# Moving 47 of 76 groups of transposes of a fused attention and token-mixing kernel from TensorE to the DMA crossbar, with a new order of the program

## The chip, the cores and the metric

One core of one Trainium2 chip. The metric is the device time of one execution in microseconds (us). Lower is better. The profile of one execution goes with each kernel; its span is 1 to 2 us shorter than the measured time.

## The reference

```python
# q, k, v: (8, 12, 448, 64) fp32;  moe_w_q, moe_w_k: (768, 64);  moe_w_out: (768, 768)
scores = q @ k.T / sqrt(64) - log(448)
x = sigmoid(scores) @ v                      # per batch and head, then heads side by side: (8, 448, 768)
wq, wk = x @ w_q, x @ w_k
W = wq @ wk.T / sqrt(64)                     # (8, 448, 448)
out = maximum(W @ x, 0) @ w_out
```

## The kernel before

Work goes by 24 "pairs": two batches by two heads. Each pair loads q, k and v (448 KB each, on SP's queue), casts them to bf16 on GpSimd (POOL), transposes q and k on TensorE (seven 128x128 blocks into PSUM, then a VectorE copy), and makes seven score blocks, each followed by one sigmoid over 128x896 on ScalarE. After six pairs the MLP of two batches follows, among the scores of the next pairs; it needs x transposed too. The order of everything is a string, one letter per step: S a score block with its sigmoid, P its product with v, q and k a transpose group, x a transpose of x, W N U M the MLP, O an output block.

```python
    def tr(n, nm, split=False):                       # q or k by TensorE
        fb, ps = bank([P, NI, 2, NP], BF16, "pt" + nm)
        t16 = ld.pop((nm + "16", n))
        for i in range(NI):
            nc.tensor.transpose(ps[:, i]..., t16[:, i]..., ident16)
        t = p_qk.tile([P, 2, NI, NP], BF16, tag=nm + "t", name=nm + "t")
        ...                                           # one VectorE copy PSUM -> t

    def pump_loads():                                 # loads: three buffers each for q, k, v
        while len(loaded) < len(ORDER):
            nm, n = ORDER[len(loaded)]
            ...
                if n >= 3 and (nm, n - 3) not in cast:
                    break
                load1(n, nm, nc.sync)
            loaded.add((nm, n))

    def pump():                                       # casts, and behind each cast the next load
        while len(cast) < len(ORDER) + 2:
            nm, n = ORDER[len(cast) - 2]
            ...
                cast1(n, nm, nc.gpsimd)
            cast.add((nm, n))
            pump_loads()
    # (cuts are marked by ...)
```

Of the kernel before, what the change touches and what calls it, by code (L numbers as in the profile page):

```python
# [9 lines left out]
F32 = mybir.dt.float32  # L10
BF16 = mybir.dt.bfloat16
# [5 lines left out]
def kernel(  # L17
# [41 lines left out]
    p_c16 = pool("c16", 2)  # L59
    p_v16 = pool("v16", 3)  # L60
    p_qk = pool("qk", 8)
# [23 lines left out]
    wqk32 = singles.tile([P, H, P], F32, name="wqk32")  # L85
# [41 lines left out]
    def tr(n, nm, split=False):  # L127
        fb, ps = bank([P, NI, 2, NP], BF16, "pt" + nm)
        t16 = ld.pop((nm + "16", n))
        for i in range(NI):  # L130
            nc.tensor.transpose(  # L131
                ps[:, i].rearrange("p h n -> p (h n)"),
                t16[:, i].rearrange("p b d -> p (b d)"), ident16,
            )
        t = p_qk.tile([P, 2, NI, NP], BF16, tag=nm + "t", name=nm + "t")

        def evac(hs):
            nc.vector.tensor_copy(  # L138
                out=t[:, hs], in_=ps[:, :, hs, :].rearrange("p i h n -> p h i n")
            )  # L140
        qk[nm, n] = t
        free1.append(fb)
        if split:
            return evac
        evac(slice(0, 2))
# [4 lines left out]
    def scores(n, i):  # L150
        fb, sc = bank2("sc")
        for b2 in range(2):
            for h in range(2):
                nc.tensor.matmul(  # L154
                    sc[HALF[h], b2, 0:S], qk["k", n][HALF[b2], h, i, :],
                    qk["q", n][HALF[b2], h].rearrange("p i n -> p (i n)"), start=True, stop=True,
                )
        at = p_at.tile([P, 2, S], BF16, tag="at", name="at")
        nc.scalar.activation(at, sc[:, :, 0:S], ACTF.Sigmoid, bias=bias_t, scale=attn_scale)  # L159
        free2.append(fb)  # L160
        ats[n, i] = at
# [21 lines left out]

    def tr_x(n):
        u, j = pairs[n]
        if j == 0:
            xns[u] = p_x.tile([P, 4, 2, D], BF16, tag="xn", name="xn")
        fb, ps = bank([P, 4, 2, 2, HD], BF16, "px")
        for h in range(2):
            for m in range(4):  # L190
                nc.tensor.transpose(  # L191
                    ps[:, m, h].rearrange("p b d -> p (b d)"), xts[j][:, h, m * P : (m + 1) * P],
                    ident16,
                )
        for b2 in range(2):
            nc.vector.tensor_copy(  # L196
                out=xns[u][:, :, b2, 2 * HD * j : 2 * HD * (j + 1)].rearrange(
                    "p m (h d) -> p m h d", h=2
                ),
                in_=ps[:, :, :, b2, :],  # L200
            )
        free1.append(fb)

# [4 lines left out]
    def mlp_wqk(u, h):  # L208

        if h == 0:  # L210
            pw[u] = bank2("pw")
        fb, ps = pw[u]
        for b2 in range(2):
            for x in range(2):
                nc.tensor.matmul(  # L215
                    ps[HALF[x], b2, 0:S], wqk16[HALF[b2], h, 64 * x : 64 * x + 64],
                    xts[h // 2][HALF[b2], h % 2, 0:S], start=(h == 0), stop=(h == H - 1),
                )
        if h == H - 1:
            nc.vector.tensor_copy(out=wqk[:, :, 0:S], in_=ps[:, :, 0:S])  # L220
            free2.append(fb)

    def mlp_wkn(u):
        fb, ps = bank([P, 4, 2, P], BF16, "pk")
        for b2 in range(2):
            for m in range(4):
                nc.tensor.transpose(ps[:, m, b2, :], wqk[:, b2, m * P : (m + 1) * P], ident16)  # L227
        wkn[u] = p_one.tile([P, 4, P], BF16, tag="wkn", name="wkn")
        nc.vector.tensor_copy(
            out=wkn[u], in_=ps.rearrange("p m b x -> p m (b x)")[:, :, 64:192]  # L230
        )
        free1.append(fb)

    def mlp_tmp(u, nb, act):
        if nb == 0:
            tmps[u] = p_one.tile([P, D], BF16, tag="tmp", name="tmp")
        fb, ps = bank([P, NB], F32, "pt")
        for m in range(4):
            for b2 in range(2):
                nc.tensor.matmul(  # L240
                    ps[HALF[b2]], wkn[u][:, m, 64 * b2 : 64 * b2 + 64],
                    xns[u][:, m, b2, nb * NB : (nb + 1) * NB],
                    start=(m == 0), stop=(m == 3),
                )
        dst = tmps[u][:, nb * NB : (nb + 1) * NB]
        if act:
            nc.scalar.copy(out=dst, in_=ps)
        else:
            nc.vector.tensor_copy(out=dst, in_=ps)
        free1.append(fb)  # L250
# [75 lines left out]
    def load_weights():  # L326
        for b2 in range(2):
            for x, w in enumerate((moe_w_q, moe_w_k)):
                o = 64 * (x ^ b2)
                nc.sync.dma_start(  # L330
                    out=wqk32[HALF[b2], :, o : o + 64], in_=w.rearrange("(h d) n -> d h n", d=HD)
                )
# [4 lines left out]


# [12 lines left out]
    nc.sync.dma_start(out=q0, in_=src["q"])  # L351
    nc.sync.dma_start(out=k0[:, :, cols(KA)], in_=src["k"][:, :, cols(KA)])
    nc.sync.dma_start(out=k0[:, :, cols(KB)], in_=src["k"][:, :, cols(KB)])
# [9 lines left out]
    fb, ps = bank2("pwarm")  # L363
    for _ in range(32):
        nc.tensor.matmul(ps[:, 0, 0:P], zeros, zeros, start=True, stop=True)
    free2.append(fb)
# [4 lines left out]
    ORDER = [("q", 1), ("k", 1), ("v", 0)]  # L371
    nq = 2
    for n in range(1, N):
        for _ in range(2 if n in (1, 2, 3, 4) else 1):
            if nq < N:
                ORDER += [("q", nq), ("k", nq)]
                nq += 1
        ORDER.append(("v", n))
    for n, at_ in ((0, 18), (1, 30), (2, 33), (3, 36), (4, 39), (5, 42), (6, 45)):
        ORDER.insert(at_, ("w", n))  # L380
# [15 lines left out]
    def pump():  # L396

        while len(cast) < len(ORDER) + 2:
            nm, n = ORDER[len(cast) - 2]
            if (nm, n) not in loaded:  # L400
                break
            if nm == "w":
                if n:
                    nc.gpsimd.tensor_copy(out=wout16[:, n - 1, :], in_=w32[n - 1])
                else:
                    nc.gpsimd.tensor_copy(out=wqk16, in_=wqk32)
            else:
                back = 3 if nm == "v" else 2
                if n >= back and (nm, n - back) not in used:
                    break  # L410
                cast1(n, nm, nc.gpsimd)
            cast.add((nm, n))
            pump_loads()
# [11 lines left out]
    for nm in "qk":  # L425
        qk[nm, 0] = p_qk.tile([P, 2, NI, NP], BF16, tag=nm + "t", name=nm + "t")

    def tr_part(nm, t16, r, e, b=None):
        shape = [P, r.stop - r.start, 2, NP]
        fb, ps = (None, ps_q.tile(shape, BF16, tag=b, name="pt" + nm)) if b else bank(shape, BF16, "pt" + nm)  # L430
        for i in range(r.start, r.stop):
            nc.tensor.transpose(
                ps[:, i - r.start].rearrange("p h n -> p (h n)"),
                t16[:, i].rearrange("p b d -> p (b d)"), ident16,
            )
        COPY[e](out=qk[nm, 0][:, :, r], in_=ps.rearrange("p i h n -> p h i n"))
# [4 lines left out]
    tr_part("q", q016, IB, "s")  # L441
    tr_part("k", k016, KA, "v", free2[-1])
    used |= {("q", 0), ("k", 0)}
    pump()





    PLAN = (  # L450
        "SSSKqSSSSkq",
        "SPPPPPSkSSPkSPqSS",
        "SxPqSPPPPSPPSqSPPSkPSPP",
        "SxPSSPkSSSkPPSkP",
        "SPPPPSqSqSSqxSxSk",
        "SSqkPPSPPPPSPqSkSSxPPPP",
        "SPPPSkqSWWWSWWWWSWWWWSWSx",
        "SNPSPPPPSPPSUSqSMUmSMq",
        "SkSMxSkSPPPSPPPPSqSk",
        "SMxmqSPPPPSPPPSOSSSOO",  # L460
        "SSkxSSOkSPPPSPPPPSO",
        "SSSqOkSPPPSPPPPSqxSPPPP",
        "SPPPSOSSSqOxSWWWWWSWW",
        "SWWWWWSOSSSNxPPPPPSPPSUU",
        "SMSxkSPPPPSPPPSOSMSkO",
        "SMmOkSMSOqSMSqOSPPPPSPPP",
        "SOSSSkOxSPPPSPPPPSxO",
        "SSSOOSSxOSPPSPPPPPPPPP",
        "SPPPSxqSWSWWWWWWSWWWSWWOS",
        "SSONSSOxSPPPPPPSPSUU",  # L470
        "SSMxOSSPPPPPPPSOSMSkx",
        "SPPPSPPPPmOSMmqOSMSOqSS",
        "SkOxSPPPPSPPPSOSSSOOx",
        "SPSPPPPPPSOSSSOOxS",
        "WPPPWPPPPWWWWWWWWWWOONxOUUMmmOOmMmOOOOOOOOOOOOOOOO",
    )
    done = dict.fromkeys("SPqkKxWNUMO", 0)
    done["q"] = done["k"] = 1

    for t in "".join(PLAN).replace(" ", ""):  # L480
        kind = "M" if t == "m" else t
# [5 lines left out]
        elif t == "P":  # L487
            n, i = divmod(c, NI)
            values(n, i)
            if i == NI - 1:  # L490
                used.add(("v", n))
                pump()
        elif t in "qk":
            tr(c, t)
            used.add((t, c))
            pump()
        elif t == "K":
            tr_part("k", k016, KB, "v")
        elif t == "x":
            tr_x(c)  # L500
        elif t == "W":
            mlp_wqk(*divmod(c, H))
        elif t == "N":
            mlp_wkn(c)
# [38 lines left out]
```

## Time and profile before

| | before |
|---|---|
| time | 210.34 us median of 2 runs (210.27 to 210.42) |
| span, granted clock of the profiled run | 209.4 us, 0.984 |
| first sigmoid starts, last one ends | 6.5 us, 177.7 us |
| ScalarE waits between them | 14.7 us, for scores (the stretch less its work; the page's own count of the waits before sigmoids, used for the other kernels below, is 12.6 us) |
| tail after the last sigmoid | 31.7 us |

The chain that ended last, by engine:

```profile
PE 75%; DMA 16%; POOL 2%; SPq 1%; ACT 1%; issue 1%; DVE 1%; DVEq 0%; ACTq 0%; POOLq 0%
```

### The profile page before, as it was taken

How to read it: one execution, taken by the hardware profiler on the slowest of the kernel's cores; microseconds unless marked ns; L12 is line 12 of the kernel's file. 1: busy time of each engine (PE TensorE's matmuls, PEld its weight loads, DVE VectorE, ACT ScalarE, POOL GpSimd, SP SyncE). 2: the span in 40 equal slices, each digit the busy share in tenths (PEclk: the TensorE clock that was granted, in tenths of full speed). 3: DMA queues.
4: the chain of work that ended last, by engine and by line, in shares of the span. 5: the costliest groups of instructions: out<-in, count | busy, mean ns of one | idle time of the engine just before them, and what ended most of it. 6: DMA issues, size and time to landing. Idle time of an engine off the chain costs nothing.

```text
span 209.4 us, 6320 instructions
## 1 busy us (share of the span) xinstructions
PE 197.0 (94%) x2630; PEld 117.5 (56%) x2630; DVE 121.9 (58%) x208; ACT 170.8 (82%) x193; POOL 72.6 (35%) x85
## 2 busy tenths in 40 slices
PE   8498988889999999999999999999999999999991
PEld 7254544556546656656656565655565555655561
DVE  2135555755598746664889675645788654554321
ACT  3689999979999999999998989889898998055220
POOL 2477755577877842730022700251110000000000
PEclk9759999999999999999999999999999999999999
DMA  5999999999999999997065463355203252154785
GB/s 174 374 381 380 381 173 290 381 384 384 383 384 383 379 381 385 399 389 253 5 199 130 145 181 79 78 147 195 51 29 78 75 152 70 27 134 104 200 203 174
DMA packets 28684, 47.59 MB, mean 227 GB/s; under 512 B 5360, under 2 KB 24432, under 8 KB 28656
## 3 DMA queue, kind: packets, MB, share of 16 engines
q1 hardware_dynamic: 27616, 45.03, 67.1%
q10 hardware_dynamic: 1040, 2.16, 2.7%
q8 instruction: 20, 0.33, 0.7%
q14 instruction: 8, 0.07, 0.1%
HBM read 36.18 MB, written 11.01 MB: 225 GB/s over the span
## 4 chain that ended last, share of the span: by engine, by line
PE 75%; DMA 16%; POOL 2%; SPq 1%; ACT 1%; issue 1%; DVE 1%; DVEq 0%; ACTq 0%; POOLq 0%
PE po L283 27%; PE sc L154 15%; PE pv L173 13%; DMA v<-in_v_dram 9%; DMA k<-in_k_dram 8%; PE px L191 5%; PE pw L215 3%; PE ptq L131 3%; PE ptk L131 3%; PE pt L240 3%; PE pm L264 2%; ACT at L159 1%; POOL k L118 1%; POOL v L118 1%; SPq L107 1%; PE pk L227 1%
## 5 line engine op out<-in xcount | busy, mean ns | idle before, releaser
L159 ACT ACTIVATE at<-sc,bias_t 128x896 bf16<-128x896 f32 x168 | 155.4, 1020 | 12.6 <-PE sc L154 11.7
L283 PE MATMUL po<-wout,mx 128*128 128x384 bf16 (+1 forms) x342 | 60.6, 324 | 0.0
L154 PE MATMUL sc<-qt,kt 64*64 64x448 bf16 x672 | 57.7, 367 | 2.5 <-ACT at L159 1.8
L283 PEld LDWEIGHTS <-mx 128*128 128x128 bf16 x342 | 30.9, 98 | 24.3 <-issue 7.0
L173 PE MATMUL pv<-at,v 64*64 64x448 bf16 x672 | 41.8, 352 | 1.1 <-POOL v L118 1.1
L178 DVE CAST xt<-pv 128x896 bf16<-128x896 f32 x24 | 26.2, 1091 | 23.4 <-PE pv L173 23.4
L308 DVE COPY o<-po 128x384 f32<-128x384 f32 x45 | 25.1, 557 | 24.7 <-PE po L283 24.4
L154 PEld LDWEIGHTS <-kt 64*64 64x64 bf16 x672 | 21.9, 105 | 23.7 <-issue 12.6
L118 POOL CAST q<-q 128x896 bf16<-128x896 f32 x23 | 21.5, 933 | 33.3 <-issue 26.3
L118 POOL CAST v<-v 128x896 bf16<-128x896 f32 x24 | 22.3, 934 | 22.6 <-PE pv L173 18.0
L118 POOL CAST k<-k 128x896 bf16<-128x896 f32 x23 | 21.5, 933 | 19.4 <-PE ptk L131 15.7
L173 PEld LDWEIGHTS <-v 64*64 64x64 bf16 x672 | 20.5, 107 | 11.2 <-POOL v L118 1.4
L138 DVE COPY kt<-ptk 128x896 bf16<-128x896 bf16 x23 | 14.3, 620 | 10.3 <-PE ptk L131 10.2
L196 DVE COPY xn<-px 128x512 bf16<-128x512 bf16 x48 | 18.0, 417 | 2.9 <-PE px L191 2.9
L306 ACT COPY o<-po 128x384 f32<-128x384 f32 x10 | 4.8, 478 | 15.7 <-PE po L283 15.7
L256 DVE TENSOR_SCALAR mx<-pm 128x896 bf16<-128x896 f32 x15 | 16.3, 1088 | 1.8 <-PE pm L264 1.4
L138 DVE COPY qt<-ptq 128x896 bf16<-128x896 bf16 x23 | 14.1, 619 | 4.5 <-PE ptq L131 3.7
L131 PE MATMUL ptq<-ident,q 128*128 128x128 bf16 x161 | 13.7, 228 | 1.4 <-POOL q L118 1.4
L191 PE MATMUL px<-ident,xt 128*128 128x128 bf16 x192 | 14.7, 220 | 0.2 <-DVE o L308 0.2
L191 PEld LDWEIGHTS <-xt 128*128 128x128 bf16 x192 | 11.6, 98 | 4.6 <-issue 3.8
L131 PE MATMUL ptk<-ident,k 128*128 128x128 bf16 x161 | 13.3, 224 | 0.6 <-POOL k L118 0.6
L131 PEld LDWEIGHTS <-q 128*128 128x128 bf16 x161 | 9.9, 102 | 6.7 <-issue 3.7
(43 smaller groups left out, 93.8 us busy)
## 6 DMA issues: line engine op xcount, KB each, us to landing
q<-in_q_dram SPq DMA_DIRECT2D x24, 448.0 KB, 8.0
v<-in_v_dram SPq DMA_DIRECT2D x24, 448.0 KB, 7.5
k<-in_k_dram SPq DMA_DIRECT2D x23, 448.0 KB, 7.8
out_dram<-o SPq DMA_DIRECT2D x44, 192.0 KB, 3.0
w<-in_moe_w_out_dram SPq DMA_DIRECT2D x6, 384.0 KB, 5.8
out_dram<-o ACTq DMA_DIRECT2D x10, 192.0 KB, 3.2
wqk<-in_moe_w_q_dram SPq DMA_DIRECT2D x2, 192.0 KB, 9.4
wqk<-in_moe_w_k_dram SPq DMA_DIRECT2D x2, 192.0 KB, 8.5
```

The costliest lines, as they stand in the source:

```text
L118: eng.tensor_copy(out=t16.rearrange("p i b d -> p b i d"), in_=ld.pop((nm, n)).rearrange("p b (i d) -> p b i d", i=NI),)
L131: nc.tensor.transpose(ps[:, i].rearrange("p h n -> p (h n)"), t16[:, i].rearrange("p b d -> p (b d)"), ident16,)
L138: nc.vector.tensor_copy(out=t[:, hs], in_=ps[:, :, hs, :].rearrange("p i h n -> p h i n"))
L154: nc.tensor.matmul(sc[HALF[h], b2, 0:S], qk["k", n][HALF[b2], h, i, :], qk["q", n][HALF[b2], h].rearrange("p i n -> p (i n)"), start=True, ...
L159: nc.scalar.activation(at, sc[:, :, 0:S], ACTF.Sigmoid, bias=bias_t, scale=attn_scale)
L173: nc.tensor.matmul(ps[HALF[b2], h, 0:S], ld["v16", n][HALF[h], i, b2, :], ats[n, i][HALF[h], b2, :], start=(i == 0), stop=(i == NI - 1),)
L178: nc.vector.tensor_copy(out=xts[j][:, :, 0:S], in_=ps[:, :, 0:S])
L191: nc.tensor.transpose(ps[:, m, h].rearrange("p b d -> p (b d)"), xts[j][:, h, m * P : (m + 1) * P], ident16,)
L196: nc.vector.tensor_copy(out=xns[u][:, :, b2, 2 * HD * j : 2 * HD * (j + 1)].rearrange("p m (h d) -> p m h d", h=2), in_=ps[:, :, :, b2, :],)
L256: nc.vector.tensor_scalar(dst, ps, moe_scale, 0.0, ALU.mult, ALU.max)
L283: nc.tensor.matmul(ps, mxs[u][c].rearrange("p b s -> p (b s)")[:, m * P : (m + 1) * P], wout16[:, c, w0:w1], start=(c == 0), stop=(c == NC ...
L308: nc.vector.tensor_copy(out=o[:, nb * NB : (nb + 1) * NB], in_=ps)
```

## The change: intent and diff

TensorE was busy 94% of the span. The change takes from it the transposes of q and k of pairs 10 to 23 (28 groups), 18 of the 24 of x, and one of the MLP's, and lets the DMA crossbar do them from SBUF to SBUF, issued by SP right behind the cast. Less TensorE and VectorE work lets the program be replanned so that ScalarE never waits. The layouts of the transposed tiles change so that one DMA can write each; two more buffers for q and k, and one more for their casts; small changes of the start (first loads in halves on two queues, dummy matmuls); the MLP's two small weights are read once in place of twice.

```diff
-    p_c16 = pool("c16", 2)
+    p_c16 = pool("c16", 3)
-    p_qk = pool("qk", 8)
+    p_qk = pool("qk", 10)
...
+    def tr_dma(n, nm):
+        t16 = ld.pop((nm + "16", n))
+        t = p_qk.tile([P, NI, P], BF16, tag=nm + "t", name=nm + "t")
+        nc.sync.dma_start_transpose(out=t, in_=t16.rearrange("p i b d -> p (i b d)"))
+        qk[nm, n] = t
...
+    def tr_x_dma(n):
+        u, j = pairs[n]
+        nc.sync.dma_start_transpose(
+            out=xn_of(u, j).rearrange("p h m x -> p (h m) x"),
+            in_=xts[j].rearrange("p h s -> p (h s)"),
+        )
...
+    BY_DMA, AHEAD = 10, 3
+    PLAN = ( ... a new string; D = dummy matmuls, X = x by DMA, n = the MLP's by DMA ... )
...
+        elif t == "S" and seen[t] % NI == 0:          # loads of q and k: three pairs ahead of the scores
+            while seen["x"] < min(N, seen[t] // NI + AHEAD + 1):
+                ORDER += [("k", seen["x"]), ("q", seen["x"])]
+                seen["x"] += 1
...
                 cast1(n, nm, nc.gpsimd)
+                if by_dma:
+                    tr_dma(n, nm)
+                    used.add((nm, n))
             cast.add((nm, n))
             pump_loads()
```

## The prediction

> **What bounds the kernel now.** I read the page first for busy shares, then the timeline of ScalarE and of TensorE, then the waits of the DMA queue, and last the groups of the operations that the change touches. Busy shares and slices of the page:
>
> ```profile
> PE 197.0 (94%) x2630; PEld 117.5 (56%) x2630; DVE 121.9 (58%) x208; ACT 170.8 (82%) x193; POOL 72.6 (35%) x85
> ...
> PE   8498988889999999999999999999999999999991
> PEld 7254544556546656656656565655565555655561
> DVE  2135555755598746664889675645788654554321
> ACT  3689999979999999999998989889898998055220
> POOL 2477755577877842730022700251110000000000
> PEclk9759999999999999999999999999999999999999
> DMA  5999999999999999997065463355203252154785
> ```
>
> Two engines lead. TensorE is never idle after slice 10. ScalarE is full from slice 4 to about 20 (21 to 105 us), then drops a tenth here and there until slice 34, where the sigmoids are over and only TensorE works. DMA is full to slice 18 (95 us), then under half. So there are three stages: a start, a long stretch in which the 168 sigmoids run, and a tail of TensorE work that needs the last sigmoids.
>
> The first and the last sigmoids, from the ScalarE timeline (start, length, engine, line, count, idle before it):
>
> ```profile
> 6.47 2.80 ACT L159 ACTIVATE at<-sc,bias_t 128x896 bf16<-128x896 f32 x3 [0.76 <-PE sc L154]
> 11.04 3.70 ACT L159 ACTIVATE at<-sc,bias_t 128x896 bf16<-128x896 f32 x4 [1.77 <-PE sc L154]
> ...
> 16.16 26.25 ACT L159 ACTIVATE at<-sc,bias_t 128x896 bf16<-128x896 f32 x29 [0.25 <-PE sc L154]
> ...
> 170.39 2.80 ACT L159 ACTIVATE at<-sc,bias_t 128x896 bf16<-128x896 f32 x3 [0.39 <-PE sc L154]
> 173.49 2.80 ACT L159 ACTIVATE at<-sc,bias_t 128x896 bf16<-128x896 f32 x3 [0.30 <-PE sc L154]
> 176.69 1.01 ACT L159 ACTIVATE at<-sc,bias_t 128x896 bf16<-128x896 f32 x1 [0.39 <-PE sc L154]
> ```
>
> The reader sees the unhindered pace in the run of 29: 26.25 / 29 = 0.905 us each. 168 of them need 152 us. They took 177.7 - 6.5 = 171.2 us. Five ReLU activations of about 0.9 us stand among them (4.5 us); the other 14.7 us is ScalarE waiting, nearly always for TensorE's scores, from 0.2 to 1.8 us at a time. From there to the end of the span are 209.4 - 177.7 = 31.7 us. So TensorE sets the time from about 85 us on, with ScalarE close behind: relieving TensorE can win those 14.7 us, and no more than that in this stretch unless ReLUs also leave ScalarE.
>
> The groups that go:
>
> ```profile
> L196 DVE COPY xn<-px 128x512 bf16<-128x512 bf16 x48 | 18.0, 417 | 2.9 <-PE px L191 2.9
> L138 DVE COPY kt<-ptk 128x896 bf16<-128x896 bf16 x23 | 14.3, 620 | 10.3 <-PE ptk L131 10.2
> L131 PE MATMUL ptq<-ident,q 128*128 128x128 bf16 x161 | 13.7, 228 | 1.4 <-POOL q L118 1.4
> L191 PE MATMUL px<-ident,xt 128*128 128x128 bf16 x192 | 14.7, 220 | 0.2 <-DVE o L308 0.2
> ```
>
> Their durations overlap in TensorE's pipeline, so I don't multiply by 220 ns. I took instead, over TensorE's timeline, the time from a group's first start to the start of the next group, less idle time: 46 complete groups of 7 q or k transposes hold TensorE 0.44 to 0.47 us each over the run (0.40 to 0.45 after 30 us, at the full clock), and a group of 8 x transposes 0.52 us.
>
> **What the Trainium skill says.** "DMA: Bandwidth & Descriptors", section Latency and other measured facts, gives a DMA transpose 261 GB/s in one kernel and 350-400 when contiguous; its section Anatomy of one DMA gives every DMA about 2 us of fixed time. From these an estimate for one 224 KB q or k (0.9 us of data) is about 3 us to landing. "VectorE: DVE Perf Modes", section The three transpose paths, has 1309 ns for one 128x128 through the crossbar against 390 ns on TensorE: alone the DMA is slower, so the change pays only if it runs ahead. No DMA transpose is in the trace of before; that row can't be checked. "DMA: Bandwidth & Descriptors", section Issuing engines are not separate DMA queues, says that all queues share the same 16 DMA engines; the trace agrees as far as it goes: plain loads at 380 GB/s take a median of 8.0 us from issue to landing, because eight are in flight at once. "TensorE: Matmul & The Clock Gate", section What's actually happening, gives half clock after an idle window of some 3.4 us; the trace agrees with 0.7 and 0.5 granted in slices 3 and 4, where TensorE had waited for loads.
>
> **The change, part by part.**
>
> TensorE loses, by instruction counts of the two builds: 196 of 336 q/k transposes (28 groups), 144 of 192 x transposes (18 groups) and 8 of 32 wkn transposes (one group). 28 x 0.44 = 12.3, 18 x 0.52 = 9.4, 0.4: together 22 us, of which one x group lay in the tail. It gains 15 dummy "D" steps of two matmuls in the start (15 x 0.19 = 2.9 us, meant to fill idle time) and 8 warming matmuls there.
>
> VectorE loses 28 x 0.62 = 17.4 us, and 48 x 0.417 = 20 us of x copies become 6 larger ones, estimated from the 620 ns for 896 columns at 0.7 us, 4 us in all. It takes over four ReLUs (4 x 1.09). It was at 58% and drops below 50%; that alone moves nothing.
>
> ScalarE loses four of nine ReLUs. Among the sigmoids one remains in place of five: 4 x 0.9 = 3.6 us off the engine that will now bind.
>
> DMA gains 28 transposes of 224 KB and 19 of 256 KB, some 11 MB, all on SP, behind their casts. The estimate above makes 28 x 0.9 + 19 x 1.0 = 44 us of DMA time, spread over the last 150 us, in which DMA is half empty. What SP pays to issue one is unknown; a plain load costs 0.37 to 0.47 us there. q and k are transposed up to three pairs ahead, some 20 us, so 3 us of latency is covered. The weights' second copy of 0.39 MB is no longer read from HBM, which frees 1 us in the loaded stage.
>
> The start: q and k of pair 0 come in halves over two queues, and the second half of k's columns no longer arrives last (it was cast only at 7.35 us, and ScalarE then idled 1.77 us). I expect the first sigmoid between 6.3 and 7 us, and about 1.5 us less idle time after it.
>
> Does TensorE then fit under the sigmoids? Before its last score at 176.2 us it had 164 us of slots from 6 us on. Less 21.5, plus 2.9 for D, less 0.8 for four P steps that now stand after the last score, plus 2 for two output blocks that now stand before it: 147 us. ScalarE's demand is 152 + 0.9 = 153 us. So the sigmoids become the bound, with TensorE 6 us under them.
>
> The sum: first sigmoid 6.6 + 153 + residual waits. TensorE is still 95% loaded relative to ScalarE and its work is lumpy (an output block of 6 matmuls holds it 0.98 to 1.08 us, more than one sigmoid), so I leave 6 of the 14.7 us of waits: last sigmoid over at about 165.6 us. Tail: 31.7 + 4 x 0.19 (P) - 2 x 0.98 (output blocks moved forward) - 0.45 (x transposes) + 0.5 (four ReLUs in a row on three PSUM buffers) = 30.5. Span 196.1; the measured time is 0.9 above the span of the profile before (210.34 against 209.4). Prediction 197.0 us, a gain of 13 us.
>
> **The rivals.**
>
> SP or the crossbar becomes the bound. For it: the skill's 1309 ns may be mostly work rather than latency. If a 128x896 transpose held the path for 4 us, 47 of them need 190 us, more than the 140 us left, and the kernel ends at 230 or more; at 2.5 us each (118 us) SP, which also issues 42 more loads and 45 stores, would be nearly full and would delay loads behind transposes, for some 203 to 210. Against it: SP's longest waits are now for output rows to be ready (48.4 us for VectorE's copies), so it has slack, and the plan uses the DMA with TensorE alternatives beside it, which looks like one tuned to a known cost.
>
> The gain is hidden anyway. If ScalarE's waits come from order and PSUM buffers, not TensorE's load, most of the 14.7 us stays and only the ReLUs (3.6), the start (1.5) and the tail (1.2) are won: 204. For it: waits of 0.25 to 0.4 us also appear while ScalarE is at 95%. Against it: from 16 to 60 us, where output blocks are absent, ScalarE hardly waits.
>
> Idle TensorE loses its clock, or a late transpose stalls a pair, most likely in the tail, where x of the last pair goes through DMA after its copy with about 5 us of other TensorE work to cover it. Each such stall costs 1 to 3 us: 199 to 201.
>
> **Range and chances.** The floor is 6.3 + 153 + 1.5 + 30 + 0.9 = 192. Rival two or several stalls give 201 to 207. So 192 to 207 in 8 of 10. Faster by over 2% means below 206.1; only a transpose path much dearer than estimated prevents it: faster 0.80, within 2% 0.10, slower 0.10.
>
> **What would show it.** In the changed kernel's profile: q/k and x transposes landing within about 3 us (right) or above 8 us with SP issue time over 2 us each (rival one); the last sigmoid ending near 165 us; ScalarE idle between sigmoids near 6 us in place of 14.7 and TensorE with visible gaps; ScalarE in the chain of waits where TensorE stood; the tail near 30.5 us. Waits of TensorE for kt, qt or xn would prove the prediction wrong, and so would unchanged ScalarE waits for scores.

## More of the kernel before

A load may start only when the cast that frees its buffer is issued, and loads, most output stores and (after the change) the transposes stand in one queue, SP's, which takes them in order.

The line of the main DMA queue on the page of before (packets, MB, share of the 16 engines' time; 67.1% of 209.4 us is 140.5 us of all 16 engines):

```profile
q1 hardware_dynamic: 27616, 45.03, 67.1%
```

And its two long stretches, by window (length, then each engine's busy time, the granted clock, the DMA share, GB/s; as the share passes 1, packets must overlap in it):

```profile
20.00:80.00 60.00, 56.80 (x863) 33.44 (x866) 38.66 (x64) 58.39 (x65) 40.58 (x44) 1.00 1.06 356
95.00:165.00 70.00, 70.00 (x991) 41.43 (x987) 48.70 (x78) 63.72 (x69) 14.38 (x16) 1.00 0.41 119
```

## The result, and the profile after

232.03 us (231.97 to 232.09, 2 runs) against 210.34: ratio 1.1031, 95% interval 1.0984 to 1.1079. Slower by 10%, where I had predicted 6% faster. (Ratios here and below are the mean time of one kernel's fast runs over that of the other's fast runs of the same rounds, so not quite the ratio of the quoted medians. The medians quoted are of all runs of a kernel; in e7, e9, e9b and h16 one of four was slow. Comparisons go by the ratios.)

The page of the changed kernel: the busy line, two rows of slices, the main DMA queue, the chain that ended last:

```profile
PE 190.8 (83%) x2320; PEld 101.6 (44%) x2320; DVE 98.9 (43%) x142; ACT 166.4 (72%) x188; POOL 73.8 (32%) x86
...
ACT  4799999999999999933269896277138899707220
...
...
DMA  6999999999999999999999999999999665792775
...
q1 hardware_dynamic: 71648, 55.79, 96.0%
...
PE 35%; DMA 29%; SPq 12%; ACT 11%; issue 5%; POOL 5%; DVE 2%; DVEq 0%; ACTq 0%; POOLq 0%
```

TensorE and VectorE did lose their work. But DMA is now full up to slice 31 (178 us), where before it was full to slice 18. Its queue carries 24% more bytes, yet takes 96.0% of 230.3 = 221.1 us of the 16 engines in place of 140.5: 80.6 us more. The chain of waits has DMA and SP's queue (SPq) in it with 41% of the span, where before it was TensorE with 75%.

ScalarE's timeline (start, length, engine, line, count, idle time before it):

```profile
38.78 58.90 ACT L156 ACTIVATE at<-sc,bias_t 128x896 bf16<-128x896 f32 x64 [0.53 <-PE sc L150]
101.51 1.90 ACT L156 ACTIVATE at<-sc,bias_t 128x896 bf16<-128x896 f32 x2 [3.84 <-PE sc L150]
...
113.46 1.91 ACT L156 ACTIVATE at<-sc,bias_t 128x896 bf16<-128x896 f32 x2 [7.18 <-PE sc L150]
...
170.10 1.01 ACT L156 ACTIVATE at<-sc,bias_t 128x896 bf16<-128x896 f32 x1 [8.27 <-PE sc L150]
...
195.22 4.65 ACT L156 ACTIVATE at<-sc,bias_t 128x896 bf16<-128x896 f32 x5 [0.29 <-PE sc L150]
```

64 sigmoids run at 0.92 us each without a break, the pace that the plan was made for, until 97.7 us. Then it breaks: waits of 4, 7 and 8 us. The last sigmoid ends at 199.9 us. The tail from there is 30.4 us.

These waits are named for TensorE's scores, but TensorE is not the one that was late. Windows of the changed kernel (columns as before):

```profile
20.00:80.00 60.00, 52.54 (x772) 28.82 (x770) 31.62 (x41) 59.20 (x67) 34.62 (x38) 1.00 1.11 298
95.00:165.00 70.00, 47.79 (x548) 23.07 (x540) 24.59 (x32) 43.04 (x46) 20.53 (x22) 0.86 1.11 266
98.00:111.00 13.00, 4.20 (x44) 1.68 (x43) 3.80 (x5) 3.81 (x4) 3.73 (x4) 0.73 1.20 239
```

From 98 to 111 us TensorE works 4.2 of 13 us, and so do the others: nobody but DMA is busy. DMA is full (1.20) while it moves only 239 GB/s; in the loaded stretch of before a full DMA moved 356. TensorE's granted clock is 0.73 there, after 1.00 from 20 to 80 us; I take that for a consequence of its idling, which no run tests.

Who waited for what (total us, times, longest):

```profile
POOL v L118 <- DMA v<-in_v_dram: 41.3, 18, 15.0
ACT at L156 <- PE sc L150: 37.4, 25, 8.3
...
DVE o L309 <- DMA out_dram<-o: 23.0, 5, 6.3
...
PE sc L150 <- DVE xt L175: 7.6, 3, 3.7
...
PE pt L241 <- DMA wkn<-wqk: 6.6, 1, 6.6
PE pt L241 <- DMA xn<-xt: 6.3, 1, 6.3
```

GpSimd's casts waited longest, for loads. But TensorE never waited for a q or k that DMA had transposed, and only 0.4 us for v. What it waited for stood behind them in SP's queue. The two longest waits of ScalarE, 8.3 us (to 170.1) and 7.2 us (to 113.5), follow TensorE's waits for two other transposes, of the MLP's wkn and of x (three of x had taken SP 7.7 us to issue). The next two, 3.8 us (to 101.5) and 3.1 us (to 147.6), follow output stores: VectorE waited up to 6.3 us for a store to free one of the three output buffers, its copy of xt stood behind that, and the scores behind the copy.

And a piece of the chain that ended last (start, length, what):

```profile
107.92 1.28 SPq L197
109.30 1.27 SPq L140
110.62 0.57 SPq L107
111.29 1.23 SPq L140
112.58 6.82 DMA q<-in_q_dram
119.55 0.94 POOL q L118
```

L197 and L140 issue transposes, L107 issues loads. Loads were late because SP first had to issue transposes; once issued, a load landed in a median of 6.2 to 6.4 us (6.8 here), no slower than in before (7.5 to 8.0). The cast waited for the load, the next transpose for the cast, and the next load, store or transpose of x stood behind that transpose in SP's queue. SP itself stood 27.4 us before transposes of q and k, waiting for casts (5.4 + 10.4 + 11.6, between 40 and 178 us; in e4, below, 2.6). The chain goes round this loop from 108 to 158 us; an output store and three transposes of x come before it (from 93.7 us), transposes of x and wkn after it (to 166.8 us). The last load of v is issued at 174.7 us, at 139.1 us in before.

What SP pays to issue (min/median/max in ns, then first and last start):

```profile
L107 SPq DMA_DIRECT2D q<-in_q_dram x23: 368/463/1432, 1.7 to 150.3; - x23
...
L140 SPq DMA_TRANSPOSE kt<-k x14: 1229/1584/2844, 50.5 to 171.5; - x14
```

A transpose costs SP at least 1.2 us, three times a plain load.

### The profile page after: what moved, and what is told of

Read it like the earlier page. It is cut to its first block, busy times and chain, and to the rows that moved or that the text cites. A ratio compares the mean times of both kernels' runs of the same rounds, so it can differ in the third digit from the quotient of the medians.

```text
span 230.3 us, 5692 instructions
## 1 busy us (share of the span) xinstructions
PE 190.8 (83%) x2320; PEld 101.6 (44%) x2320; DVE 98.9 (43%) x142; ACT 166.4 (72%) x188; POOL 73.8 (32%) x86
## 2 busy tenths in 40 slices
DMA packets 72970, 58.77 MB, mean 255 GB/s; under 512 B 49872, under 2 KB 68688, under 8 KB 72944
## 4 chain that ended last, share of the span: by engine, by line
PE 35%; DMA 29%; SPq 12%; ACT 11%; issue 5%; POOL 5%; DVE 2%; DVEq 0%; ACTq 0%; POOLq 0%
PE po L284 17%; ACT at L156 11%; DMA v<-in_v_dram 10%; DMA k<-in_k_dram 9%; PE sc L150 6%; PE pv L170 6%; DMA q<-in_q_dram 6%; SPq L197 5%; SPq L140 3%; SPq L107 3%; DMA out_dram<-o 2%; PE pw L213 2%; PE pt L241 2%; POOL v L118 2%; DMA wkn<-wqk 1%
## 5 line engine op out<-in xcount | busy, mean ns | idle before, releaser
L150 PE MATMUL sc<-qt,kt 64*64 64x448 bf16 x672 | 63.1, 375 | 12.9 <-DVE xt L175 7.6
L284 PEld LDWEIGHTS <-mx 128*128 128x128 bf16 x342 | 30.5, 98 | 32.4 <-issue 16.3
L257 DVE TENSOR_SCALAR mx<-pm 128x896 bf16<-128x896 f32 x19 | 20.7, 1092 | 4.8 <-PE pm L265 4.8
L241 PE MATMUL pt<-xn,wkn 128*64 128x384 bf16 x64 | 8.8, 411 | 13.0 <-DMA wkn<-wqk 6.6
L250 DVE CAST tmp<-pt 128x384 bf16<-128x384 f32 x7 | 3.9, 556 | 20.2 <-PE pt L241 20.2
L213 PE MATMUL pw<-xt,wqk 64*64 64x448 bf16 x192 | 12.4, 382 | 0.2 <-DVE xt L175 0.2
L241 PEld LDWEIGHTS <-wkn 128*64 128x64 bf16 x64 | 3.7, 131 | 17.3 <-DMA wkn<-wqk 6.9
L133 DVE COPY kt<-ptk 128x896 bf16<-128x896 bf16 x9 | 5.6, 624 | 11.3 <-PE ptk L131 11.3
L265 PE MATMUL pm<-wqk,tmp 64*64 64x448 bf16 x96 | 8.6, 375 | 1.6 <-ACT at L156 1.0
L213 PEld LDWEIGHTS <-wqk 64*64 64x64 bf16 x192 | 7.0, 114 | 3.1 <-issue 0.4
L218 DVE CAST wqk<-pw 128x896 bf16<-128x896 f32 x4 | 4.4, 1091 | 8.3 <-PE pw L213 8.3
```

Of the source, the lines that this page charges most:

```text
L150: nc.tensor.matmul(sc[HALF[h], b2, 0:S].rearrange("p (i n) -> p i n", i=NI), qk["k", n][HALF[b2], i, HALF[h]], qk["q", n][HALF[b2], :, HAL ...
L213: nc.tensor.matmul(ps[HALF[x ^ b2], b2, 0:S], wqk16[HALF[b2], h, 64 * x : 64 * x + 64], xts[h // 2][HALF[b2], h % 2, 0:S], start=(h == 0), ...
L241: nc.tensor.matmul(ps[HALF[b2]].rearrange("p (x d) -> p x d", d=HD), wkn[u][:, b2, m, HALF[1 - b2]], xns[u].rearrange("p j h m x -> p (j h ...
L257: nc.vector.tensor_scalar(dst, ps, moe_scale, 0.0, ALU.mult, ALU.max)
L265: nc.tensor.matmul(ps[HALF[x], b2, 0:S], tmps[u][HALF[b2], c * P + 64 * x : c * P + 64 * x + 64], wqk[HALF[b2], b2, 0:S], start=True, stop ...
L284: nc.tensor.matmul(ps, mxs[u][c].rearrange("p b s -> p (b s)")[:, m * P : (m + 1) * P], wout16[:, c, w0:w1], start=(c == 0), stop=(c == NC ...
```

## The experiments

Three theories. A: the transposes' own work on the 16 DMA engines is dearer than I had estimated, and loads starve. B: SP, one queue in order, is held by issuing them. C: the new order is at fault, whoever transposes. A and B can both be true; the last runs divide them. Kernels that compute wrong values are marked.

### The transpose by itself (m1_alone, wrong)

Twelve transposes of 128x896 bf16, then twelve loads of 448 KB, then twelve plain copies of the same 224 KB, then loads and transposes by turns; each phase waits for the one before.

> Measures the disputed cost alone (wrong result on purpose: the kernel only moves data). Four phases, each behind a gate: 12 crossbar transposes of 128x896 from SP, 12 plain loads of 448 KB, 12 plain SBUF-to-SBUF copies of the same 224 KB, then 12 loads alternating with 12 transposes. Theory A (a transpose occupies the 16 DMA engines): about 1.6 us per transpose also when alone, since the changed kernel shows 896 packets of 256 B at 28.8 ns over 16 engines; a copy about 0.6 us; mixed phase about the sum, 12 x (1.6 + 1.2) = 34 us. Theory B (a transpose costs little on the engines, its packets only look long because loads run beside them, and its price is SP's issue of 1.25 us): 12 transposes take 15 us, packets alone are well under 20 ns, and the mixed phase is far shorter than the sum.

SP's timeline of m1_alone, then its windows of the transposing and of the copying phase (the last two columns are DMA share and GB/s):

```profile
1.82 16.08 SPq L60 DMA_TRANSPOSE dst<-src  x12
...
38.83 7.69 SPq L63 DMA_DIRECT2D dst<-src  x12
```

```profile
2.00:20.00 18.00, 0.66 (x2) 0.00 (x0) 1.00 0.80 153
...
38.80:48.60 9.80, 0.01 (x1) 0.00 (x0) 1.00 0.76 281
```

A stream of transposes goes at 16.08 / 12 = 1.34 us each, with the engines 0.80 busy and 153 GB/s moved over the window; 0.80 x 18 / 12 makes 1.2 us of the engines each. Plain copies of the same bytes take half as long. With a load between them a load and a transpose take 2.33 us together ((74.91 - 49.29) / 11, from SP's timeline), while a load alone is 1.17 us of data at the 390 GB/s that the page has for the loads. That is 93% of the sum of 1.34 and 1.17. So the price is more than my 0.9 us of DMA time, and a transpose hides hardly at all behind a load. The expectation is split: twelve alone took close to the 15 us of B, and not 1.6 us each as A had it; the mixed phase is near the sum of its parts, as A had it, though not at its 34 us. (One run, its state unknown.) That alone explains neither 33 us nor which of the two resources it is.

### The new order with all transposes on TensorE (e1_all_pe)

```diff
-                    tr_dma(n, nm)                  # and the same for x and the MLP's
+                    later(8, lambda: tr(n, nm))    # on TensorE, a few steps behind the cast
```

> The changed kernel with every transpose back on TensorE, order and loads kept (q and k of pair 10 on are transposed eight steps after their cast, x and wkn a few steps after the place of their DMA). If the DMA transposes are the cause (theories A and B): 203 to 214 us. If the new order and its later casts are the cause (theory C): it stays above 222 us.

223.56 us, ratio 1.0599 (1.0565 to 1.0633). TensorE is full from 80 us on (79.34 of 80 us between 80 and 160), and ScalarE waits 25.8 us (12.6 in before). The order is made for a TensorE without these transposes and costs 13 us with them. By the expectation this is C's number, above 222, and not the 203 to 214 of A and B: I had thought that the order alone cost less. But this does not show that the order costs anything where TensorE is relieved. The next run asks that.

### Plain copies in place of transposes (e4_plain, wrong)

```diff
-        nc.sync.dma_start_transpose(out=t, in_=t16.rearrange("p i b d -> p (i b d)"))
+        nc.sync.dma_start(out=t.rearrange("p i x -> p (i x)"), in_=t16.rearrange("p i b d -> p (i b d)"))
```

All 47 in this way: same queue, same bytes, same waits, same order.

> Every DMA transpose of the changed kernel becomes a plain SBUF-to-SBUF copy of the same bytes on the same queue at the same place (wrong result on purpose). Waits, order and number of DMAs stay. Theory A: DMA time falls by some 50 us and the kernel comes to the time that was predicted, 196 to 204 us. Theory B (the in-order SP queue, where a transpose waits for its cast and holds loads and stores behind it): most of the loss stays, 215 us or more, as the waits are the same; only the shorter issue gives something back.

199.15 us (198.85 to 201.0), ratio 0.9462 (0.9414 to 0.9511). Slices and queue on its page, then ScalarE's timeline:

```profile
DMA  6999999999999998999999999999654575336875
...
q1 hardware_dynamic: 32368, 55.78, 84.1%
```

```profile
16.76 96.76 ACT L156 ACTIVATE at<-sc,bias_t 128x896 bf16<-128x896 f32 x105 [0.34 <-PE sc L150]
```

105 sigmoids without a break, ScalarE waits of 6.1 us in all (12.6 in before), the last sigmoid over at 166.6 us, span 197.1. C falls: with the new order and cheap transfers the kernel would be 5% faster than before. The difference from the changed kernel, 33 us, is the price of transposing instead of copying. The time is the one expected under A, and it refutes B as that text has it, that the queue's waits alone keep the loss. But a plain copy is also cheaper for SP to issue (0.47 us at least, against 1.22), so SP's time and the engines' are not yet divided. DMA takes 84.1% of 197.1 = 165.8 us here, 55 us less than with transposes.

One trap shows here. The plain copies take a median of 4.8 to 6.1 us from issue to landing, the transposes of the changed kernel 4.6 to 5.7. Landing times are the same in the kernel that runs well and in the one that doesn't. It is the rate that differs, not the latency.

### Half of the transposes (e2_x_only, e3_qk_only)

The new order; in e2 only x by DMA (q, k on TensorE as in e1), in e3 only q and k.

> Only x goes through DMA transposes (18 of them); q, k and the last wkn are back on TensorE. Theory A (DMA engine time): 28 x 1.6 = 45 us of DMA time leave, TensorE gets back 28 x 0.44 = 12.3 us, so DMA is no longer full and TensorE, at about 160 us before the last score, binds: 206 to 216 us. If the latency of the x transposes in the path of the mixer is what hurts, whatever DMA's load, ScalarE stalls of 4 to 8 us stay at the two places where the mixer starts, and the time stays above 220.

> Only q and k of pair 10 on go through DMA transposes (28); x and wkn are back on TensorE. Theory A: 19 x 1.84 = 35 us of DMA time leave, TensorE gets back 9.8 us: 204 to 214 us. If head-of-line waiting on SP behind the q and k transposes is the cause, little is won: 222 us or more.

e2: 212.84 and 213.02 us in its two fast runs (two were slow, 216.43 and 365.70 us; in the second, the profiled one, TensorE went at about half pace throughout, six matmuls of an output block in 2.11 us where they hold it about 1 us before, so its profile is not used), ratio 1.0124 (1.0068 to 1.018). e3: 212.99 (212.06 to 215.21), ratio 1.0142 (1.0073 to 1.0211). Both within the expected ranges; at 2% e2 counts as the same as before, e3 is unclear. Either half gives back 10 of the 13 us that the order cost in e1; the two together cost 8 to 9 more than e1 alone. So neither kind of transpose is bad by itself: it takes both, and these runs do not show whether by their number or by where they stand.

### The loads on another queue (e5_pool_loads)

```diff
-                load1(n, nm, nc.sync)
+                load1(n, nm, nc.gpsimd if late else nc.sync)   # late: q, k from pair 10 on, v from pair 6 on
```

> The loads of q and k from pair 10 on and of v from pair 6 on are issued by GpSimd, whose casts free their buffers, in place of SP; transposes and stores stay on SP. Theory A: unchanged within 3%, 225 to 238 us, as the bytes and packets stay. Theory B: loads no longer stand behind transposes, 205 to 216 us.

270.6 and 272.2 us in its two fast runs (the two slow ones 284.1 and 293.0), ratio 1.2868: neither number. It was meant to take SP's order out of the way and brought in something worse. With loads running that GpSimd had issued, the issue of one transpose held SP 18.09 us (from 93.20 us, L140). This run tells nothing about the split between A and B. It shows only that another queue is no way out here.

### Changing one of SP time and packet size

The profile's packet counts differ by kind: with transposes, 49872 of 72970 packets are under 512 B; with plain copies, 4576 of 33690. So a plain copy cut into 256-byte pieces gives the DMA engines the transposes' packets without the crossbar. Time of SP alone can be added with drain instructions behind each plain copy: they hold SP and add no transfer.

First two attempts, both plain copies. Their outputs are wrong, which doesn't matter for the times. e7 makes three copies of each; e8 makes one, in 256-byte pieces (a destination padded by 16 columns):

```diff
-        nc.sync.dma_start(out=t, in_=t16)                         # e4, shortened
+        for a, b in ((0, 3), (3, 5), (5, 7)):                     # e7
+            nc.sync.dma_start(out=t[:, a:b], in_=t16[:, a:b])
+        t = p_qk.tile([P, NI, P + 16], ...)[:, :, 0:P]            # e8
+        nc.sync.dma_start(out=t, in_=t16)
```

> Every DMA transpose becomes three plain copies of a third of the bytes each (wrong result on purpose), so that SP spends about 3 x 0.45 = 1.3 us on it, as on a transpose, while the DMA engines move the bytes at the plain rate. If SP's issue time is what costs: as the changed kernel, 220 to 232. If occupancy of the DMA engines is what costs: within 2% of the single plain copies, 197 to 203.

> Every DMA transpose becomes one plain copy whose destination blocks are padded, so that it is cut into 256 B pieces as a transpose is (wrong result on purpose); SP issues it in one go, about 0.45 us. If many small packets on the DMA engines are what costs (the trace shows 28.8 ns for 256 B): 218 to 235 us. If it is SP's issue time, or something that only the crossbar does: 197 to 206.

e7: 240.48 us (238.8 to 242.4), ratio 1.1465, slower than the changed kernel, with the main queue at only 76.4% of the engines. So engines need not be full for a loss. But it has 94 more DMAs, each with its own completion to wait for, so its size isn't to be compared, and it is above either expectation. e8: 217.23 us (215.7 to 218.6), ratio 1.0327 (1.026 to 1.0394), just under the 218 to 235 expected if packets cost: 256-byte pieces bring back over half of the loss. But each also takes SP 0.60 us at least, against 0.47.

Then the drains. e9: e4 with sixteen drains behind each copy; e9b: with nine; e10: e8 with eight.

```diff
         nc.sync.dma_start(out=t, in_=t16)                         # e4 or e8, shortened
+        [nc.sync.drain() for _ in range(9)]
```

> Wrong values on purpose: e4 (every transpose replaced by one plain copy of the same bytes) with sixteen drain instructions on SP behind each copy, which adds time of SP and nothing to DMA. How long sixteen take is what this run measures first. If SP's issue time is what costs the time, then at about 0.8 us more per copy (47 x 0.8 = 38 us) it goes from e4's 199 towards 220-232 with DMA busy no more than in e4; if the DMA engines' occupancy by the transposes is the cost, it stays at 199-204.

> Wrong values on purpose. As e9, with nine drains behind each copy in place of sixteen. Sixteen held SP for 1.30 us, so nine hold it 0.73 us: with the copy's own 0.47 us that is the 1.2 us that a transpose takes on SP at least. SP time is then that of the transposes and the DMA engines' work that of plain copies. If SP time is all of the loss: 225-232. In proportion to e9 (199 to 218 for 1.30 us): 208-211. If it only bites above what SP can spare: 200-206.

> Wrong values on purpose. e8 (each transpose replaced by one plain copy in 256-byte pieces, 0.60 us on SP at least, 217 us in all) with eight drains, about 0.65 us, behind each copy: SP time and packet size are now those of the transposes, without the crossbar. If the two together are the whole loss: 227-235 (the changed kernel has 232). If the crossbar adds something of its own: 217-225.

The holds were measured in SP's timeline, from the end of one copy's issue to the next start: 1.30 us with sixteen, 0.94 us with nine, 0.89 us with eight. So nine held longer than the 0.73 us I had scaled from sixteen, and a copy of e9b takes SP 1.41 us. That is above a transpose's least 1.22 us and close to its median of 1.42 (x) to 1.58 us (q, k). The main queue of e9b, then of e8, then of e10:

```profile
q1 hardware_dynamic: 32368, 55.78, 82.1%
```

```profile
q1 hardware_dynamic: 70896, 55.78, 88.7%
```

```profile
q1 hardware_dynamic: 70896, 55.78, 86.5%
```

| kernel | SP per copy, about | pieces | ratio to before (95%) | in us, x 210.3 | engines' time on q1 |
|---|---|---|---|---|---|
| e4 plain | 0.5 us | 1792 B and more | 0.946 (0.941 to 0.951) | 199.0 | 165.8 us |
| e9b, nine drains | 1.4 us | as e4 | 0.987 (0.978 to 0.997) | 207.6 | 169.3 us |
| e9, sixteen drains | 1.8 us | as e4 | 1.034 (1.027 to 1.042) | 217.5 | 170.0 us |
| e8 | 0.6 us least, 0.65 to 0.9 median | 256 B | 1.033 (1.026 to 1.039) | 217.2 | 192.3 us |
| e10, eight drains | 1.5 us | 256 B | 1.068 (1.062 to 1.074) | 224.6 | 192.5 us |
| changed kernel | 1.2 us least, 1.4 to 1.6 median | 256 B | 1.103 (1.098 to 1.108) | 232.0 | 221.1 us |

(The runs of this table are from several chips, so the ratios are compared. The last column is the page's share times its span.)

Differences between rows of this table are good to about 2 us, by the intervals. e9b and e9 show B by itself: hardly more work for the DMA engines (169 to 170 us against 165.8), and 9 and 18 us lost against e4. (e9 at 218.07 us and e9b at 207.99 lie just under the ranges expected if SP's time were all, 220 to 232, and in proportion, 208 to 211.) e8 shows mainly A: 18 us lost. Both together, e10, lose 25.6 us, close to 9 + 18. The whole loss is 33 us, so some 7 us are left for the crossbar itself: neither SP time nor packet size brings them, as far as these runs match both. The last column fits that, transposes keep the engines busy 28.6 us longer than plain 256-byte pieces do. The packet records of the kept traces show where: a 256-byte packet took 28.8 ns on average in the changed kernel and 19.6 in e8, while the median is 18 ns in both, so it is a few of the transposes' packets that take much longer (one in a hundred over 127 ns, in e8 over 45). I have no run that lets me put exactly those 7 us down to it. The expectation for e10 named 227 to 235 if nothing but the two counted and 217 to 225 if the crossbar adds its own: 224.12 us is in the second.

### Fewer transposes, in the order of before (h0, h16, h16x, h12x, hx, h18x)

All parts of the change but the order, with the order of before. h0: all on TensorE (a control). The others by DMA: h16, q and k of pairs 16 to 23; h16x, these and eight x; h12x, q and k of pairs 12 to 23 and ten x; hx, ten x only; h18x, q and k of pairs 18 to 23 and eight x.

```diff
-    BY_DMA, AHEAD = 10, 3
-    PLAN = ( ... the new order ... )
+    BY_DMA, AHEAD, X_DMA = 18, 7, (13, 14, 15, 16, 18, 19, 20, 21)     # h18x
+    PLAN = ( ... the order of before ... )
```

> Control for the next three: the order of the kernel before (its step list, load order and casts) with everything else of the change (start in halves on two queues, packed layouts, one x copy in place of two, one read of the weights), and every transpose on TensorE. If the order is what makes the version with all transposes on TensorE slow (223.6 us): 206 to 211 us here. If the new layouts or the start cost something: 214 or more.

> As the control, with q and k of pairs 16 to 23 by DMA transpose behind their casts (16 of them), at about 105 us and later, where DMA of the kernel before was 40% busy and SP 54%. TensorE loses 16 x 0.44 = 7 us; DMA gains 16 x 1.6 = 26 us in a stretch with room. If the loss of the change is queue and engine time in the loaded stage: 201 to 206 us. If a DMA transpose hurts wherever it is placed: 210 or more.

> As the one before, with eight of the last eleven x transposes by DMA too: TensorE loses 4.2 us more, DMA gains 15 us. By queue and engine time: 198 to 204 us. If x, which is in the path of the mixer, can't bear the landing time of 4 to 5 us: slower than the one before.

> As the one before, with q and k from pair 12 on (24 of them) and ten x by DMA. TensorE would lose 15.8 us against the control, but transposes begin at about 80 us, while loads still fill DMA. If DMA and SP have room only after about 100 us: no better than the one before, 200 to 210 us; if the amount of transposes alone counted, 196 to 200.

> The order of before, only the ten x of pairs 12 to 21 by crossbar, no q or k. If the engines' occupancy is what makes transposes dear, ten of them behind the loads (which are over by then in this order) cost nothing and free TensorE of ten groups of 0.52 us: 205-209. If any transpose on SP delays the rest: 210-213.

> The order of before, q and k of pairs 18 to 23 and eight x by crossbar: four transposes fewer than h16x (208.91 us). If a few more or fewer transposes in the emptier second half decide, 207-210; nothing here is expected to be faster than before by 2%.

| kernel | transposes by DMA | us | ratio to before (95%) | DMA full to about |
|---|---|---|---|---|
| h0 | 0 | 210.67 | 1.0000 (0.9949 to 1.005) | 94 us |
| hx | 10 | 209.34 | 0.9945 (0.9892 to 0.9997) | 93 us |
| h16 | 16 | 212.97 | 1.0068 (0.9992 to 1.0144) | 131 us |
| h18x | 20 | 207.78 | 0.9869 (0.9818 to 0.9921) | 139 us |
| h16x | 24 | 208.91 | 0.9925 (0.9868 to 0.9982) | 145 us |
| h12x | 34 | 228.22 | 1.0824 (1.0768 to 1.088) | 159 us |

The control is as fast as before, as expected: the other parts (start, layouts, buffers) move nothing by themselves, within 0.5%. Its main queue:

```profile
q1 hardware_dynamic: 25520, 44.18, 66.4%
```

Of the five expectations that followed, h18x's held and hx ended 0.3 us above its better range. h16 came out on the side of "hurts wherever it is placed" (210 or more, not 201 to 206); h16x (198 to 204, or slower than h16) and h12x (200 to 210, or 196 to 200) missed. Up to 24 transposes, of which those of q and k start at 70 us or later and those of x at 100 us or later, do little; with 34, the first at 50 us, the same break appears as in the changed kernel (ScalarE waits 11.02 us at one place, to 104.6 us; VectorE had waited up to 12.1 us there for an output store). So a limit stands between 24 and 34 transposes with this order; since h12x also starts them 20 us earlier, among the loads, it is not shown whether the number or the place makes it. h18x, 1.3% faster than before, is the best correct kernel and beats both, though not by 2%. Why h16, with fewer transposes than h16x, gains nothing is open.

## Why the prediction was wrong

By its own steps:

- **First sigmoid at 6.3 to 7 us**: 7.1, just outside, and later than the 6.5 of before.
- **TensorE loses 22 us, and fits under the sigmoids with 6 us of waits**: right in kind, but visible only where transfers are cheap. e4 has 105 sigmoids in a row and 6.1 us of waits by the page's count (12.6 in before by the same count). The 22 us are not measured as such: TensorE's busy time falls by 15.1 us there (197.0 to 181.9), dummies included. And in e4's chain TensorE still has 63% and ScalarE 22%, so ScalarE did not take its place.
- **Last sigmoid over at 165.6 us; tail 30.5; span 196.1**: 166.6, 30.5 and 197.1 in e4. In the changed kernel the tail is 30.4, but the last sigmoid ends at 199.9 us. Of the miss of 35 us, 34 lie before that point, nearly all of them after 97.7 us, up to which 97 sigmoids run within 1 us of e4's.
- **"28 x 0.9 + 19 x 1.0 = 44 us of DMA time, spread over the last 150 us, in which DMA is half empty"**: this is the step that failed, in both halves. Against the control h0 (66.4% of 208.1 = 138.2 us of engine time, no transposes) the changed kernel has 221.1 us: 83 us for 47 transposes, 1.76 us each, nearly twice the estimate. (Plain copies: 165.8 - 138.2 = 28 us.) This is the time that packets took, and it is the transposes' own: by the packet records of the trace, their 44544 packets of 256 bytes took some 80 us of it, while the loads' packets of 1792 bytes took 86 ns each on average against 81 in h0. Alone, in m1_alone, a transpose took 1.2 us of the engines, still above the estimate. And DMA was half empty only from 95 us on, in the order of before. The new order loads q and k three pairs ahead of the scores and no further, so loads run beside the transposes: in e4, without the crossbar's price, the last q is loaded at 119.5 us in place of 92.9, and DMA is full to 138 us. I took the space from the old kernel's profile and the traffic from the new one.
- **"What SP pays to issue one is unknown"**: left out of the sum, at a cost. It is 1.2 us at least, and e9b shows that SP time of that order costs 9 us in this plan.
- **"3 us of latency is covered by three pairs ahead, some 20 us"**: true of q and k: they land in about 5 us, as plain copies do, and TensorE never waited for one. (The 3 us counted a fixed 2 us whose source speaks of DMAs that GpSimd issues.) But x and wkn are not issued ahead, and output stores have three buffers. All stand in SP's queue behind the transposes of q and k, and from 97.7 us on they came late. The prediction had said that waits of TensorE for xn would prove it wrong: there is one of 6.3 us, and one of 6.6 us for wkn.
- **Rival one, SP or the crossbar becomes the bound**: this is what happened, at a time (232 us) that I had tied to 4 us per transpose. About 1.5 us of SP and 1.76 us of the engines sufficed, because both are shared with loads that already fill DMA. I had argued against it that SP waits long for output rows, so it has slack. But waits of an in-order queue at one place are no slack at another: a load behind a transpose can't use them. The sign that I had named for this rival, landing above 8 us and SP over 2 us each, did not show: 4.6 to 5.7 and 1.4 to 1.6 us.
- **Rival two, ScalarE's waits come from order and PSUM buffers**: no. In e4 they halve, as predicted.
- **Rival three, idle TensorE loses its clock or a late transpose stalls a pair, 1 to 3 us each**: the late transposes came true, at 6.3 and 6.6 us and not in the tail. The lower clock (0.73 from 98 to 111 us) went with the idling.
- **Three readings of the trace were wrong, with little weight for the sum**: the clock of 0.7 and 0.5 is in the second and third slice, not the third and fourth, and TensorE's longest single wait there was 1.2 us, so an idle window of 3.4 us is not what this trace shows. And 8.0 us of landing time at 380 GB/s makes six to seven loads of 448 KB in flight, not eight. And the run profiled before took 211.18 us, so its time is 1.8 us above its span, not 0.9.
- **"a plan that looks like one tuned to a known cost"**: not evidence. Only h18x and its like, with fewer transposes, are near a cost that pays.

The chance of 0.10 for slower was too low for a sum whose largest new term rested on no row of the trace.

What stays open: why a few of the transposes' packets take so long, and whether they make the last 7 us, and the exact share of SP and of the engines, since SP's issue took longer among loads (in m1_alone 1.23 to 2.27 us, against 1.34 on average alone), so the two need not be independent.

## What to carry to other kernels

Before work is moved to DMA, add up the DMA engines' time in the new order, with the measured time of that kind of transfer, and do the same for the queue that issues it; bytes over bandwidth is not enough, and empty slices of the old profile may not be empty in the new one. Behind a queue that takes things in order, the victim need not be what was moved: q and k were never late here, output stores and x were. So follow each long wait back to the DMA that ended it, and look at what stood before that DMA in its queue. To price an operation in place, exchange it for a cheaper one with the same waits, even at the price of wrong values: one such run separated the order from the transposes.

## What the Trainium skill lacked or had wrong

- "DMA: Bandwidth & Descriptors", section Latency and other measured facts, gives DMA transposes 261 GB/s and 350-400 in the contiguous case. Transposes of 128x896 bf16 from SBUF to SBUF, contiguous, alone on one queue, ran at 1.34 us for 224 KB, that is 171 GB/s (153 over the window with its ends). The engines were 0.80 busy then, so SP's issue may set that pace; at 1.2 us of the engines each it would be 191 GB/s. My 0.9 us came from that row.
- "Advanced Engine Details and Errata", section X-Bar Transpose (TRN2), says that transpose DMAs are as fast as regular ones. In these runs 47 transposes in place of 47 plain copies of the same bytes cost 33 us (232.0 against 199.2 us).
- No page gives, as a time on this chip, what the issuing engine pays for a DMA of each kind ("DMA: Bandwidth & Descriptors" has only sequencer cycles for earlier generations, in a part on a later chip). Here it was 1.22 us at least for a transpose on SP, 0.37 us at least and 0.47 us in the median for a plain load.
- I found no page that warns of what e5 showed: loads on GpSimd's queue beside transposes on SP held the issue of one transpose 18.09 us.
